# A planned order for windowed attention and a gated feed-forward layer: ScalarE's exponentials and tanh freed of each other, the plan's ranks searched again

## The chip, the cores and the metric

The kernel runs on one core of one Trainium2 chip. The metric is the device time of one execution in microseconds (us). A core has five engines that work at the same time, each through its own instructions in their given order: TensorE (PE in the profile, with PEld for its weight loads), VectorE (DVE), ScalarE (ACT), GpSimd (POOL) and SyncE (SP, which here issues the DMAs).

## The reference

Eight sequences of 576 tokens pass through attention with 8 heads of 64 and a window of 64 keys, and then through a feed-forward layer whose hidden part is gated by its own convolution.

```python
scores = scale * np.matmul(q, k.transpose(0, 1, 3, 2))
mask = (rel >= 0) & (rel < window)
scores = np.where(mask, scores, -1000000000.0)
attn = np.exp(scores - np.max(scores, axis=-1, keepdims=True))
attn = attn / (np.sum(attn, axis=-1, keepdims=True) + 1e-09)
x = np.matmul(attn, v)              # heads side by side: 512 columns
h = np.maximum(x @ w_in, 0.0)       # 512 -> 1024
conv_out = sum(conv_w[k] * hp[:, k:k + S, :] for k in range(3))
gate = 1.0 / (1.0 + np.exp(-conv_out))
return (h * gate) @ w_out           # 1024 -> 512
```

The weights come as 64-bit floats and are made into 32-bit ones on the chip. Each operand of the two large products is split into a high and a low part, and a product is made of three matmuls: high by high, low by high and high by low.

## The kernel before

**Units.** The 4608 tokens are cut into 12 units of 384 (`NU`, `NX`). A unit passes through attention (scores, exponentials, values), then the first product for 8 slices f of 128 hidden columns (`mm1`, line 547: 12 matmuls a slice), ReLU (lines 573 and 576), the convolution and its gate for pairs of slices (`conv_mid` 582, `conv_side` 589, `sig` 596, `gate` 601, `gate_hi` 613, `gate_lo` 616), and the second product (`mm2`, line 625: 9 matmuls a slice, three for each block of 128 tokens), after which the result is copied out of PSUM (lines 679 and 681) and stored.

**Attention.** `qk` (line 375) makes the scores with small matmuls on parts of the array; `row_max` (382, DVE) masks them and takes the maxima; `exps` (392, ACT) takes the exponentials with their sums; `guard`, `reciprocal` and `normalise` (395, 398, 403) divide. For units 0 and 1 the probabilities are transposed by PE (`transpose_pe` 408, copied out by `untile` 413), for the later ones by DVE (429) and DMAs (441). `values` (527) multiplies by v, again with small matmuls, one work for each of four slices c; `split_hi` (531, ACT) and `split_lo` (534, DVE) make the two parts that `mm1` reads.

**Weights.** w_in and w_out come in slices of 512 KB (line 273, into `bits`, which has four places). `to_f32` rebuilds a slice with ACT (259 and 264) and DVE (260, 261 and 265); `weights` then splits it (280 or 282, and 283). w_in is converted as slices 0, 1, (2,3), (4,5), (6,7), w_out as (0,1), (2,3), (4,5), (6,7).

**The planner.** The order on each engine isn't written out; `queued` (lines 67 to 143) works it out when the program is built. Every piece of work is a `Work` with an engine, a cost in us, what it reads and writes, and a rank `t`. The planner keeps a clock for each engine. At each step it takes the engine that can start first, and of that engine's ready works the one of lowest rank; a work of the same `kind` as the one before it on its engine counts as 0.5 lower. Ranks count steps of the first product: unit u's slice f has rank n = 8u + f, and a negative rank stands ahead of unit 0. Unit u's second product of slice f has rank n + lag + 0.5; each row of `START["sig"]`, `["pv"]`, `["qk"]` and `["ex"]` gives, relative to 8u, the ranks of unit u's gates, of unit u+1's values, and of unit u+2's scores and exponentials. The last row of each holds for all later units. The numbers in `START` are found by a search over the planner's clock, and they decide the order alone: on the chip, an engine goes on as soon as its next instruction's data is there.

**Kinds.** On PE the small matmuls of scores and values are "tiled" (units 0 and 1, and all values) or "eight" (scores from unit 2 on), and going in or out costs `SWITCH["PE"]` or `LEAVE`. On ACT, exponentials are of kind "exp" and tanh of kind "sig". A change costs 1.28 us on the planner's clock, and lines 741 to 745 add a name "table" to what these works read or write, so that no exponential crosses a tanh in either direction.

**Filling.** Where the planner sees PE idle before 110 us it adds matmuls on a zero tile (`keep_busy`, line 222), as many as fit in the gap by its clock. Their results are not used.

**The first loads.** `load_qk` for unit 0 issues four pairs of loads of k and q (two groups of heads g, each cut in two along the tokens, a = 0 and 1; line 245), all of one rank, `START["qk0"][0] - 1` = -98.8. The loads of ranks below that are w_in's slice 0 (-258.9) and the convolution's weights (-180.9, line 304).

Of the kernel before, what the change touches and what calls it, by code (L numbers as in the profile page):

```python
# [31 lines left out]
NB = 4  # L32
# [34 lines left out]
def queued(works, fill=None):  # L67
# [30 lines left out]
    dma, port, order, left = 0.0, {"DVE": 0.0, "POOL": 0.0}, [], len(works)  # L98
    while left:
# [29 lines left out]
        end = free[e] = start + turn + x.cost * (1.75 if e == "PE" and start < WARM else 1.0)  # L129
# [18 lines left out]
    "v0": -71.95,  # L148
    "pv0": -34.655,
    "conv": -180.897,  # L150
    "bits": ((-258.913, -43.524), (-27.85, -45.73)),
    "qk1": -49.157,
    "lag": (14.24, 14.398, 15.694, 15.676, 15.748, 15.604),
    "mid": (34.105, 23.924, 1.179, 2.877),
    "v1": -14.571,
    "qk2": 1.159,
    "qk0": (-97.809, -91.941, -91.937, -96.905, -77.255, -53.129),
    "ex0": (5.091, -53.0, -51.19, -48.925, -20.5, -38.281),
    "sc1": (-39.624, -39.363, -29.157, -27.618, -17.395, 0.944),
    "ex1": (-174.932, -9.707, -5.699, 0.394, -22.941, 2.774),  # L160
    "mask": -65.788,
    "sig": ((11.177, 14.758, 14.533, 18.236), (11.894, 12.691, 15.861, 19.769), (14.354, 16.018, 17.085, 17.977), (13.566, 14.937, 17.862, 18.669)),
    "in": (-109.707, -10.794, -9.091, -3.35, 0.324),
    "out": (1.022, 7.827, 9.957, 12.645),
# [9 lines left out]
COLD = 5.4  # L174


@with_exitstack
def attention_moe(ctx: ExitStack, tc: tile.TileContext, q, k, v, w_in, conv_w, w_out, out):
# [76 lines left out]
    def to_f32(t, n, st, x, kb, kt):  # L255
# [3 lines left out]
        at(t, "ACT", 0.0009 * n + 0.2, lambda: nc.scalar.activation(x, hw.bitcast(F32), AF.Abs, scale=2.0 ** -112), r=kb, w=kt)  # L259
        two(t, "DVE", 0.00052 * n + 0.06, lambda: nc.vector.tensor_scalar(xu, xu, 3, None, op0=ALU.logical_shift_left), w=kt)  # L260
# [3 lines left out]
        at(t, "ACT", 0.0009 * n + 0.2, lambda: nc.scalar.activation(lw, lw, AF.Copy, scale=2.0 ** -29), w=kb)  # L264
        two(t, "DVE", 0.00104 * n + 0.07, lambda: nc.vector.tensor_tensor(xu, xu, lw, ALU.add), r=kb, w=kt)  # L265

    def weights(t, src, fs, hi, lo, key, buf, halves):
# [11 lines left out]
        if key == "out":  # L279
            at(t, "ACT", 0.0009 * n + 0.12, lambda: nc.scalar.copy(hi, x), r=kt, w=his)  # L280
        else:
            two(t, "POOL", 0.00127 * n, lambda: nc.gpsimd.tensor_copy(hi, x), r=kt, w=his)
# [180 lines left out]
    def weigh(u, ns, t):  # L463

        bis = [divmod(2 * n + i, NB) for n in ns for i in range(2)]
        for b, i in bis:
            at(t, "ACT", 0.78, lambda b=b, i=i: exps(u, b, i), r=[("nm", b, i)], w=[("s", b, i), ("sm", b, i)], kind="exp")
# [5 lines left out]
        at(t, "DVE", 0.15, lambda: reciprocal(b, e), r=sw, w=[("r", b, i) for _, i in bis])  # L473
        two(t, "DVE", 0.05 + 0.275 * len(bis), lambda: normalise(u, b, e, nc.vector), r=[("r", b, i) for _, i in bis], w=sr)
        for n in ns:
            m, g = [("po", PE_AT[u][n])], 2 * n // NT
            at(t + 0.4, "PE", 0.66, lambda n=n: transpose_pe(u, n), r=[("s", b, n % 2 * 2), ("s", b, n % 2 * 2 + 1), "mask0"], w=m)
            at(t + 0.5, "ACT", 0.55, lambda n=n: untile(u, n), r=m, w=[("u", g, i) for i in range(4)])

    def softmax(u, b, t, ex_at):  # L480
# [18 lines left out]
        at(t, "DVE", 0.15, lambda: reciprocal(b, e), r=sw, w=[("r", b, i) for i in range(NB)])  # L499
# [217 lines left out]
    for u in range(NU):  # L717
# [4 lines left out]
        for c, x in enumerate(START["pv"][min(u, 3)]):  # L722
            attend(u + 1, c, n0 + x)
# [84 lines left out]
```

## Time and profile before

| | |
|---|---|
| median of 3 runs | 508.27 us (508.21 to 508.46) |
| profiled execution | 508.16 us |
| its span, first to last instruction | 506.4 us |
| granted TensorE clock, mean | 1.0 |
| read from and written to HBM | 47.73 and 9.44 MB, 113 GB/s over the span |

The span is what the trace covers. The profiled execution took 1.76 us more than its span and 0.11 us less than the median. In the rows, L547 is line 547 of the kernel; an entry such as "acc<-xh,wih" names what is written and what is read; "x384" is a count. A PE row "issue" is time in which PE waited for nothing that the profile shows.

### The profile page before, as it was taken

The numbers are of one execution on the slowest core, as the hardware profiler recorded it, in microseconds if no ns is written. First come the engines' busy times: TensorE is split into PE (matmuls) and PEld (weight loads), VectorE is DVE, ScalarE is ACT, GpSimd is POOL, SyncE is SP. The second block draws the span as 40 slices with busy tenths as digits, with TensorE's granted clock in tenths as the row PEclk, the third lists the DMA queues.
The fourth block names the chain that finished last, engine by engine and source line by source line (L and its number), as shares of the span: only waits on it lengthen the run. The fifth ranks groups of instructions, "written<-read, shape, count | busy, mean of one in ns | idle before, by whom it ended". The sixth has DMA issues, their size and how long they took to land.

```text
span 506.4 us, 14083 instructions
## 1 busy us (share of the span) xinstructions
PE 497.4 (98%) x5452; PEld 446.8 (88%) x5452; DVE 370.8 (73%) x1079; ACT 338.0 (67%) x975; POOL 94.1 (19%) x196
## 2 busy tenths in 40 slices
PE   8999999999999999999999998999999999999997
PEld 7888998988989989988989997998998998999886
DVE  4899999798687667767867666685877775454980
ACT  5999988768768648647747755854864864444750
POOL 7125412401121402102200400220220320000000
PEclk9999999999999999999999999999999999999999
DMA  8985833528128226316415522722720521100111
GB/s 294 380 312 204 329 119 112 222 73 322 32 64 293 79 64 244 113 48 212 160 48 168 195 57 82 274 54 81 276 61 15 190 66 29 63 0 1 63 63 62
DMA packets 28162, 69.88 MB, mean 138 GB/s; under 512 B 5696, under 2 KB 15680, under 8 KB 28096
## 3 DMA queue, kind: packets, MB, share of 16 engines
q1 hardware_dynamic: 27952, 68.86, 39.8%
q8 instruction: 43, 0.70, 0.6%
q14 instruction: 23, 0.19, 0.1%
q10 hardware_dynamic: 144, 0.13, 0.1%
HBM read 47.73 MB, written 9.44 MB: 113 GB/s over the span
## 4 chain that ended last, share of the span: by engine, by line
PE 91%; DVE 4%; ACT 2%; issue 1%; DMA 1%; SPq 0%; POOL 0%; ACTq 0%; POOLq 0%
PE acc L547 39%; PE po L625 39%; PE acc L527 7%; PE sc L375 3%; PE acc L375 2%; ACT s L392 2%; DVE s L382 1%; DMA q<-in_q_dram 1%; DVE T L261 1%; PE sc L625 1%; DVE T L265 0%; ACT ub L413 0%; DVE xl L534 0%; DVE T L260 0%; DVE wil L283 0%
## 5 line engine op out<-in xcount | busy, mean ns | idle before, releaser
L589 DVE SCALAR_TENSOR_TENSOR c<-hbuf,cw,c 128x384 f32<-128x384 f32 (+1 forms) x192 | 116.8, 659 | 28.2 <-ACT c L582 27.5
L547 PE MATMUL acc<-xh,wih 128*128 128x384 f32 x384 | 130.9, 341 | 1.0 <-DVE nm L382 1.0
L547 PE MATMUL acc<-xl,wih 128*128 128x384 f32 x384 | 129.4, 337 | 0.0
L547 PE MATMUL acc<-xh,wil 128*128 128x384 f32 x384 | 129.0, 336 | 0.0
L625 PE MATMUL po<-woh,gh 128*128 128x512 f32 (+1 forms) x288 | 113.3, 393 | 0.0
L625 PE MATMUL po<-wol,gh 128*128 128x512 f32 (+1 forms) x288 | 112.5, 391 | 0.0
L625 PE MATMUL po<-woh,gl 128*128 128x512 f32 (+1 forms) x288 | 111.1, 386 | 0.0
L392 ACT ACTIVATE s<-s,nm 128x96 f32<-128x96 f32 (+2 forms) x288 | 105.1, 371 | 3.9 <-DVE nm L382 3.9
L547 PEld LDWEIGHTS acc<-xh,wih 128*128 128x128 f32 x384 | 72.1, 188 | 6.1 <-DVE nm L382 1.0
L576 ACT ACTIVATE hbuf<-acc 128x384 f32<-128x384 f32 x64 | 31.3, 492 | 65.5 <-PE acc L547 65.5
L547 PEld LDWEIGHTS acc<-xh,wil 128*128 128x128 f32 x384 | 72.1, 188 | 2.7
L403 POOL TENSOR_TENSOR s<-s,r 128x768 f32<-128x768 f32 x27 | 42.9, 1590 | 159.7 <-DVE r L398 124.9
L547 PEld LDWEIGHTS acc<-xl,wih 128*128 128x128 f32 x384 | 72.1, 188 | 0.0
L625 PEld LDWEIGHTS po<-woh,gl 128*128 128x128 f32 x288 | 54.1, 188 | 11.8
L625 PEld LDWEIGHTS po<-woh,gh 128*128 128x128 f32 x288 | 54.0, 187 | 9.3
L625 PEld LDWEIGHTS po<-wol,gh 128*128 128x128 f32 x288 | 54.2, 188 | 7.3
L601 DVE SCALAR_TENSOR_TENSOR c<-c,hbuf 128x768 f32<-128x768 f32 (+1 forms) x48 | 50.3, 1048 | 11.8 <-ACT c L596 11.5
L582 ACT ACTIVATE c<-hbuf,cw 128x384 f32<-128x384 f32 (+1 forms) x96 | 53.7, 609 | 4.9 <-DVE gl L616 4.9
L392 ACT ACTIVATION_READ_ACCUMULATOR s<-s,nm 128x1 f32 x288 | 55.4, 192 | 0.0
L616 DVE TENSOR_TENSOR gl<-c,gh 128x768 fp32r<-128x768 f32 x48 | 45.6, 950 | 12.8 <-ACT gh L613 12.6
L613 ACT CAST gh<-c 128x768 fp32r<-128x768 f32 x48 | 39.9, 834 | 22.3 <-DVE c L601 13.4
L527 PEld LDWEIGHTS acc<-ub,v 128*64 128x64 f32 x1152 | 36.2, 138 | 8.3 <-issue 6.0
(76 smaller groups left out, 547.2 us busy)
## 6 DMA issues: line engine op xcount, KB each, us to landing
v<-in_v_dram SPq DMA_DIRECT2D x24, 768.0 KB, 6.2
ub<-T SPq DMA_DIRECT2D x240, 48.0 KB, 1.9
k<-in_k_dram SPq DMA_DIRECT2D x22, 448.0 KB, 6.3
q<-in_q_dram SPq DMA_DIRECT2D x22, 384.0 KB, 6.5
out_dram<-T SPq DMA_DIRECT2D x11, 768.0 KB, 3.6
bits<-in_w_in_dram SPq DMA_DIRECT2D x8, 512.0 KB, 8.2
bits<-in_w_out_dram SPq DMA_DIRECT2D x8, 512.0 KB, 4.8
k<-in_k_dram SPq DMA_DIRECT2D x2, 256.0 KB, 4.7
```

The lines of the kernel that those rows point to most:

```text
L375: nc.tensor.matmul(bank_of(u, b, i, h)[r:r + rows, o:n], qs[hs, 2 * g + p, t:t + rows], ks[hs, 2 * g + p, t + o:t + n], start=True, stop=True)
L392: nc.scalar.activation(x, x, AF.Exp, bias=nms[b][:, e], scale=-1.0, accum_out=sms[b][:, e])
L403: on.tensor_tensor(sv, sv, rs[b][:, e].unsqueeze(2).broadcast_to([P, e.stop - e.start, n]), ALU.mult)
L527: nc.tensor.matmul(acc[bank(("v", u, c))][h * D:(h + 1) * D, t * W:(t + 1) * W], vs[:, c, t, h], ub[g][:, 2 * p:2 * p + 2, 2 * t + h], sta ...
L547: nc.tensor.matmul(acc[bank(("m", u, f))][:, :NX], w[:, f, c], x[u % 2][:, c], start=(c == 0 and j == 0), stop=(c == NC - 1 and j == 2))
L576: nc.scalar.activation(hbuf[:, f, 1:1 + NX], ps[:, :NX], AF.Relu, scale=0.5)
L582: nc.scalar.activation(cs[i % 2][:, a, :n], hbufs[u % 2][:, f, 1:1 + n], AF.Copy, scale=cw[:, 1, f:f + 1])
L589: nc.vector.scalar_tensor_tensor(c, hbufs[u % 2][:, f, e:e + n], cw[:, e, f:f + 1], c, op0=ALU.mult, op1=ALU.add)
L601: nc.vector.scalar_tensor_tensor(c, c, 1.0, hbufs[u % 2][:, 2 * i:2 * i + 2, 1:1 + n], op0=ALU.add, op1=ALU.mult)
L613: nc.scalar.copy(halves(u, ghs[ring(u, i)]), kept(u, cs[i % 2]))
L616: nc.vector.tensor_tensor(halves(u, gls[ring(u, i)]), kept(u, cs[i % 2]), halves(u, ghs[ring(u, i)]).bitcast(F32), ALU.subtract)
L625: nc.tensor.matmul(ps[:, :e.stop - e.start], x, w[:, f, e], start=(f == 0 and j == 0), stop=(f == NF - 1 and j == 2))
```

## The change

It has four parts.

1. Exponentials and tanh lose their kinds. The 1.28 us for a change and the "table" dependencies are gone from the plan, so that exponentials, tanh and gates may stand in any order on ACT.
2. The planner's clock learns of PE's supply of instructions: small matmuls use up a store (`FEED`, `FEED_CAP`), which fills at `FEED_RATE`; a work that finds too little lasts longer on the planner's clock.
3. The four pairs of first loads of k and q get a rank each (`START["first"]`).
4. Costs of works are set to durations nearer to the trace, and all ranks are searched anew. `sig`, `pv`, `ex` and `qk` get a fifth row each and `mid` a fifth entry.

No work is added or taken away: each instruction of the reference's computation stays, in another place of its engine's order. The number of filling matmuls can change.

```diff
@@ queued
-    dma, port, order, left = 0.0, {"DVE": 0.0, "POOL": 0.0}, [], len(works)
+    dma, fed, fed_at = 0.0, FEED_CAP, 0.0
+    port, order, left = {"DVE": 0.0, "POOL": 0.0}, [], len(works)
...
-        end = free[e] = start + turn + x.cost * (1.75 if e == "PE" and start < WARM else 1.0)
+        end = start + turn + x.cost * (1.75 if e == "PE" and start < WARM else 1.0)
+        if e == "PE" and x.kind:
+            n, supply = FEED[x.kind] * x.cost, FEED_RATE if start < 95 else 3.0
+            fed = min(FEED_CAP, fed + (start - fed_at) * FEED_RATE)
+            end += max(0.0, (n - fed - supply * (end - start)) / FEED_RATE)
+            fed, fed_at = max(0.0, fed + (end - start) * supply - n), end
+        free[e] = end
@@ START
-    "v0": -71.95,
-    "conv": -180.897,
-    "bits": ((-258.913, -43.524), (-27.85, -45.73)),
-    "lag": (14.24, 14.398, 15.694, 15.676, 15.748, 15.604),
-    "mid": (34.105, 23.924, 1.179, 2.877),
-    "sig": ((11.177, 14.758, 14.533, 18.236), (11.894, 12.691, 15.861, 19.769), (14.354, 16.018, 17.085, 17.977), (13.566, 14.937, 17.862, 18.669)),
-    "in": (-109.707, -10.794, -9.091, -3.35, 0.324),
-    "out": (1.022, 7.827, 9.957, 12.645),
-    "pv": ((6.465, 3.218, 3.982, 6.814), (5.391, 7.651, 7.7, 7.657), (4.506, 6.705, 6.851, 6.707), (5.736, 6.769, 6.475, 6.894)),
-    "qk": ((4.51, 3.967, 5.895), (7.399, 7.175, 7.913), (5.253, 4.827, 5.309), (5.703, 5.416, 6.817)),
+    "v0": -96.077,
+    "first": (-137.786, -116.075, -136.572, -107.669),
+    "conv": -81.327,
+    "bits": ((-96.451, -86.268), (-79.16, -73.986)),
+    "lag": (14.497, 13.78, 14.414, 14.455, 15.373, 15.868),
+    "mid": (17.91, 0.125, 1.189, 3.534, 0.816),
+    "sig": ((12.866, 11.647, 14.331, 16.917), (12.693, 14.451, 17.624, 16.371), (12.581, 15.72, 15.39, 17.641), (12.826, 14.888, 15.551, 18.095), (11.686, 15.325, 16.648, 19.92)),
+    "in": (-24.305, -20.754, -9.713, -6.689, -3.697),
+    "out": (-2.439, -0.767, 9.791, 13.159),
+    "pv": ((3.969, 6.795, 4.159, 6.958), (7.28, 7.239, 7.367, 7.68), (6.46, 6.532, 6.657, 6.788), (6.325, 6.971, 6.181, 6.599), (6.49, 6.675, 6.478, 6.731)),
+    "qk": ((0.694, 3.909, 10.137), (7.309, 6.673, 8.272), (3.708, 3.714, 7.013), (2.788, 2.736, 6.609), (3.334, 3.026, 6.693)),
...
+FEED, FEED_CAP, FEED_RATE = {"tiled": 33, "eight": 78}, 150.0, 12.0
@@ load_qk
             for a in range(len(CUTS[g])) if u == 0 else (0,):
+                t = START["first"][2 * g + a] if u == 0 else t
@@ to_f32, weights: costs
-        at(t, "ACT", 0.0009 * n + 0.2, lambda: nc.scalar.activation(x, hw.bitcast(F32), AF.Abs, scale=2.0 ** -112), r=kb, w=kt)
-        two(t, "DVE", 0.00052 * n + 0.06, lambda: nc.vector.tensor_scalar(xu, xu, 3, None, op0=ALU.logical_shift_left), w=kt)
+        at(t, "ACT", 0.0009 * n + 0.11, lambda: nc.scalar.activation(x, hw.bitcast(F32), AF.Abs, scale=2.0 ** -112), r=kb, w=kt)
+        two(t, "DVE", 0.00045 * n + 0.08, lambda: nc.vector.tensor_scalar(xu, xu, 3, None, op0=ALU.logical_shift_left), w=kt)
...
@@ weigh (softmax in the same way)
-            at(t, "ACT", 0.78, lambda b=b, i=i: exps(u, b, i), r=[("nm", b, i)], w=[("s", b, i), ("sm", b, i)], kind="exp")
+            at(t, "ACT", 0.78, lambda b=b, i=i: exps(u, b, i), r=[("nm", b, i)], w=[("s", b, i), ("sm", b, i)])
...
@@ moe
-            s = n0 + START["sig"][min(u, 3)][i]
-            m = max(n + 0.4 if u % 3 == 2 else n + NF + 0.4, s - START["mid"][min(u, 3)])
+            s = n0 + START["sig"][min(u, 4)][i]
+            m = max(n + 0.4 if u % 3 == 2 else n + NF + 0.4, s - START["mid"][min(u, 4)])
...
-            at(s, "ACT", 0.75, lambda i=i: sig(u, i), w=[c], kind="sig")
-            two(s + 0.05, "DVE", 0.92, lambda i=i: gate(u, i), r=hs, w=[c])
+            at(s, "ACT", 0.75, lambda i=i: sig(u, i), w=[c])
+            two(s + 0.05, "DVE", 0.875, lambda i=i: gate(u, i), r=hs, w=[c])
...
@@ the plan's first lines
-    load_qk(START["qk0"][0] - 1, 0)
+    load_qk(None, 0)
```

The ranks of `qk0`, `ex0`, `sc1`, `ex1`, `pv0`, `v1`, `qk1`, `qk2` and `ex` change as well.

More of the change, by code (lines that the diff above doesn't have):

```diff
@@ L279, in weights @@
         if key == "out":
-            at(t, "ACT", 0.0009 * n + 0.12, lambda: nc.scalar.copy(hi, x), r=kt, w=his)
+            at(t, "ACT", 0.00088 * n + 0.05, lambda: nc.scalar.copy(hi, x), r=kt, w=his)
         else:
-            two(t, "POOL", 0.00127 * n, lambda: nc.gpsimd.tensor_copy(hi, x), r=kt, w=his)
+            two(t, "POOL", 0.00105 * n, lambda: nc.gpsimd.tensor_copy(hi, x), r=kt, w=his)
         two(t, "DVE", 0.00104 * n + 0.07, lambda: nc.vector.tensor_tensor(lo, x, hi.bitcast(F32), ALU.subtract), r=kt + his, w=los)
@@ L472, in weigh @@
         at(t, "POOL", 0.6, lambda: guard(b, e, nc.gpsimd), w=sw)
-        at(t, "DVE", 0.15, lambda: reciprocal(b, e), r=sw, w=[("r", b, i) for _, i in bis])
+        at(t, "DVE", 0.12, lambda: reciprocal(b, e), r=sw, w=[("r", b, i) for _, i in bis])
         two(t, "DVE", 0.05 + 0.275 * len(bis), lambda: normalise(u, b, e, nc.vector), r=[("r", b, i) for _, i in bis], w=sr)
@@ L477, in weigh @@
             at(t + 0.4, "PE", 0.66, lambda n=n: transpose_pe(u, n), r=[("s", b, n % 2 * 2), ("s", b, n % 2 * 2 + 1), "mask0"], w=m)
-            at(t + 0.5, "ACT", 0.55, lambda n=n: untile(u, n), r=m, w=[("u", g, i) for i in range(4)])
+            at(t + 0.5, "ACT", 0.47, lambda n=n: untile(u, n), r=m, w=[("u", g, i) for i in range(4)])
     def softmax(u, b, t, ex_at):
@@ L490, in softmax @@
             at(t, "ACT", 0.74, lambda b=b, i=i: exps(u, b, i), r=[("nm", b, i)],
-               w=[("s", b, i), ("sm", b, i)], kind="exp")
+               w=[("s", b, i), ("sm", b, i)])
         t += 0.45
@@ L498, in softmax @@
             at(t, "DVE", 0.15, lambda: guard(b, e, nc.vector), w=sw)
-        at(t, "DVE", 0.15, lambda: reciprocal(b, e), r=sw, w=[("r", b, i) for i in range(NB)])
+        at(t, "DVE", 0.12, lambda: reciprocal(b, e), r=sw, w=[("r", b, i) for i in range(NB)])
         if u < 3:
@@ L537, in attend @@
         g, x = c // 2, u % 2
-        at(t, "PE", 0.72, lambda: values(u, c), r=[("v", g)] + [("u", g, i) for i in range(4)], w=[("acc", ("v", u, c))],
+        at(t, "PE", 0.735, lambda: values(u, c), r=[("v", g)] + [("u", g, i) for i in range(4)], w=[("acc", ("v", u, c))],
            kind="tiled")
-        at(t + 0.1, "ACT", 0.4, lambda: split_hi(u, c), r=[("acc", ("v", u, c))], w=[("xh", x, c)])
+        at(t + 0.1, "ACT", 0.375, lambda: split_hi(u, c), r=[("acc", ("v", u, c))], w=[("xh", x, c)])
         at(t + 0.2, "DVE", 0.48, lambda: split_lo(u, c), r=[("acc", ("v", u, c)), ("xh", x, c)], w=[("xl", x, c)])
@@ L638, in moe @@
                    w=[("acc", ("m", u, f))])
-            at(n + 0.3, "ACT", 0.4, lambda f=f: relu(u, f), r=[("acc", ("m", u, f))], w=[("h", y, f)])
+            at(n + 0.3, "ACT", 0.385, lambda f=f: relu(u, f), r=[("acc", ("m", u, f))], w=[("h", y, f)])
             for o in range(TT):
@@ L678, in moe @@
             if o % 2 == 0 or u < 2:
-                at(t + 0.05 * o, "ACT", 0.55, lambda o=o: nc.scalar.copy(ot[:, o], po[o]), r=[("po", o)], w=ob)
+                at(t + 0.05 * o, "ACT", 0.475, lambda o=o: nc.scalar.copy(ot[:, o], po[o]), r=[("po", o)], w=ob)
             else:
-                at(t + 0.05 * o, "DVE", 0.65, lambda o=o: nc.vector.tensor_copy(ot[:, o], po[o]), r=[("po", o)], w=ob)
+                at(t + 0.05 * o, "DVE", 0.61, lambda o=o: nc.vector.tensor_copy(ot[:, o], po[o]), r=[("po", o)], w=ob)
             if u == LAST:
@@ L721, in attention_moe @@
             break
-        for c, x in enumerate(START["pv"][min(u, 3)]):
+        for c, x in enumerate(START["pv"][min(u, 4)]):
             attend(u + 1, c, n0 + x)
         if u + 2 < NU:
-            for b, (x, y) in enumerate(zip(START["qk"][min(u, 3)], START["ex"][min(u, 3)])):
+            for b, (x, y) in enumerate(zip(START["qk"][min(u, 4)], START["ex"][min(u, 4)])):
                 softmax(u + 2, b, n0 + x, n0 + y)
```

26 lines of the change are left out of this document (13 added, 13 removed), and 2 rows, old and new, of the table START.

## The prediction

> **What bounds the kernel now.** I read the page's busy shares and slices first, then the busy times by stretch, then the chain of work that ended last.
>
> ```profile
> PE 497.4 (98%) x5452; PEld 446.8 (88%) x5452; DVE 370.8 (73%) x1079; ACT 338.0 (67%) x975; POOL 94.1 (19%) x196
> ...
> DVE  4899999798687667767867666685877775454980
> ```
>
> PE is busy 98% of the span of 506.4 us, and DVE only 73%, but DVE's slices (12.66 us each) stand at 9 from the third to the seventh. So the start has another limit than the rest. The stretches show it; behind each window and its length stand the busy us of PE, PEld, DVE, ACT and POOL:
>
> ```profile
> 7.00:25.00 18.00, 17.70 (x273) 15.83 (x274) 15.80 (x67) 16.47 (x61) 6.10 (x24) 1.00 1.02 386
> 25.00:47.00 22.00, 20.44 (x387) 17.72 (x387) 21.89 (x101) 20.86 (x73) 8.30 (x11) 1.00 0.74 256
> 47.00:90.00 43.00, 42.52 (x534) 39.07 (x536) 42.90 (x102) 38.57 (x105) 12.33 (x21) 1.00 0.57 198
> 90.00:105.00 15.00, 15.00 (x93) 14.16 (x89) 11.07 (x37) 11.03 (x40) 5.81 (x8) 1.00 0.50 174
> 320.00:460.00 140.00, 139.98 (x1300) 126.28 (x1299) 93.55 (x228) 84.00 (x224) 19.61 (x42) 1.00 0.28 91
> ```
>
> And two of the stretches for line 222 alone, the filling matmuls:
>
> ```profile
> 7.00:25.00 18.00, 8.47 (x62) 7.33 (x62) 1.00 1.02 386
> 25.00:47.00 22.00, 2.24 (x12) 1.70 (x12) 1.00 0.74 256
> ```
>
> From 7 to 47 us PE is idle 0.30 + 1.56 = 1.86 us and fills 8.47 + 2.24 = 10.71 us: 12.6 us without real work. From 320 to 460 it is idle 0.02 us of 140. The work of PE is fixed, so what can be won lies before 47 us, and in single gaps. In the start DVE sets the pace: between 25 and 90 us it is idle 0.11 + 0.10 = 0.21 us of 65. Only behind 90 us is it loose (3.93 us idle of 15). PE runs through from 47 us on because the first products of units 0 and 1 lie ready; it meets DVE again where the second product begins:
>
> ```profile
> 74.89 0.66 DVE L260 TENSOR_SCALAR T<-T 128x1024 uint32<-128x1024 uint32 x1
> ...
> 76.35 0.93 DVE L616 TENSOR_TENSOR gl<-c,gh 128x768 fp32r<-128x768 f32 x1
> 77.18 1.22 DVE L261 SCALAR_TENSOR_TENSOR T<-bits,T 128x1024 uint32<-128x1024 uint32 x1
> ...
> 80.71 1.23 DVE L265 CUSTOM_DVE_ANT_0 T<-bits,T 128x2048 uint16<-128x2048 uint16 x1
> ...
> 83.77 1.24 DVE L283 TENSOR_TENSOR wol<-T,woh 128x1024 fp32r<-128x1024 f32 x1
> ```
>
> ```profile
> 78.37 2.06 PE po L625 x9
> ...
> 105.22 2.06 PE po L625 x9
> ```
>
> The first gate is done at 76.35 + 0.93 = 77.28, and the chain of waits has its matmuls at 78.37: 1.1 us of slack. An earlier PE is worth nothing unless DVE delivers earlier too.
>
> **The change part by part.** *First loads.* The SP queue and the end of the first wait:
>
> ```profile
> 0.74 0.38 SPq L273 DMA_DIRECT2D bits<-in_w_in_dram  x1
> 1.18 0.41 SPq L304 DMA_DIRECT2D cbits<-in_conv_w_dram  x1
> 1.64 0.43 SPq L245 DMA_DIRECT2D k<-in_k_dram  x1
> 2.12 0.47 SPq L245 DMA_DIRECT2D q<-in_q_dram  x1
> ```
>
> ```profile
> 2.12 4.14 DMA q<-in_q_dram
> ...
> 6.39 0.56 PE sc L375 x16
> ```
>
> The new ranks put g0's first pair ahead (-137.8), then g1's first pair (-136.6), then the second pairs, then w_in's slice 0 (-96.45), v, and the rest. The first q takes SP's second place: issued at about 1.2 instead of 2.12, 0.9 us earlier. It also has less ahead of it: no 512 KB of weights. Those landed, issued at 0.74, when ACT began on them:
>
> ```profile
> 4.27 0.67 ACT L259 ACTIVATE T<-bits 128x512 f32<-128x512 f32 x1 [2.25 <-DMA bits<-in_w_in_dram]
> ...
> 4.97 0.43 DVE L260 TENSOR_SCALAR T<-T 128x512 uint32<-128x512 uint32 x1 [3.97 <-ACT T L259]
> ...
> 5.46 0.68 DVE L261 SCALAR_TENSOR_TENSOR T<-bits,T 128x512 uint32<-128x512 uint32 x1
> ...
> 7.82 0.75 DVE L265 CUSTOM_DVE_ANT_0 T<-bits,T 128x1024 uint16<-128x1024 uint16 x1
> ```
>
> That is 3.5 us from issue. k and q of the first pair are smaller, so I take 3.4, a landing at 4.6 instead of 6.26: 1.6 us won (bounds 0.9, the issue alone, and 2.1). In return slice 0's conversion loses its place. It now runs in DVE's empty time before the scores; its rank goes from -109.7 to -24.3, between the first exponentials. DVE's 0.43 + 0.68 + 0.75 = 1.86 us then fall where it has 18.00 - 15.80 = 2.2 us of idle time (7 to 25 us), which may or may not lie in the right places: cost 0 to 1.9, taken as 0.9, the middle, since I see nothing that decides. Net: **-0.7 us**, bounds -2.1 and +1.0.
>
> *The order on DVE and ACT to 105 us.* The last conversion of w_out (the four rows of 74.89 to 83.77) takes 0.66 + 1.22 + 1.23 + 1.24 = 4.35 us of DVE and is done at 85.01, yet its slices 6 and 7 are first used at 105.22. In the old ranks it (12.645) stands ahead of the tanh of unit 0's second pair (14.758); in the new ones that tanh (11.647) stands ahead of it (13.159). This is where the freed order counts: tanh need not stand behind exponentials of lower rank. Moving those 4.35 us behind what PE waits for could win up to 3.9 us, the room that DVE has from 90 to 105. Against it: w_out's first two conversions go from 1.022 and 7.827 to -2.439 and -0.767, which brings DVE work ahead that no PE work before 78 us needs. The first of them is early already:
>
> ```profile
> 55.20 1.18 DVE L283 TENSOR_TENSOR wol<-T,woh 128x1024 fp32r<-128x1024 f32 x1
> ```
>
> It ends 22 us ahead of its use; so I let half of one conversion (2.2 us) be the loss at worst. I take **-2.5 us**, nearer to the first end, since the last conversion stands 20 us too early in the rows and PE's 12.6 us leave room for it; bounds -3.9 and +2.2. The other moved ranks of the start, those of the second unit's softmax and of the later loads on SP among them, are inside these bounds: the DMA engines are full from 7 to 25 us (share 1.02) and no longer behind (0.74), and the one wait for weights by ACT is the 2.25 us above. The freeing itself takes no instruction away: the chip changes no tables.
>
> ```profile
> L259 ACT ACT_TABLE_LOAD x1 | 1.3, 1283 | 0.7 <-PEq L797 0.7
> ```
>
> One load of 1283 ns serves all exponentials and tanhs, so the planner's 1.28 us for each change was never there to win.
>
> *Spacings on PE.* Two gaps of the chain fall inside bursts of small matmuls:
>
> ```profile
> 54.44 0.35 issue
> ...
> 307.27 1.31 issue
> ```
>
> At 307 us a softmax's pair of score works (128 matmuls) and one values work (24) run in one burst, and it stops at its end; at 54 us it is 72 and 64. The new clock charges for such bursts and the ranks are searched under that charge. I take **-1.5 us** of the 1.66, bounds -1.66 and 0; the other side is a rival. The stops go with the supply of instructions:
>
> ```profile
> q8 instruction: 43, 0.70, 0.6%
> ```
>
> Here the Trainium skill (Runtime: NRT & Kernel Launch, Instruction fetch mechanics) says that instructions come in blocks of 16 KiB (256 instructions), and that crossing into the next is mostly hidden. The block agrees: 0.70 MB in 43 packets is 16 KB, and twice 5452 PE rows over 43 is 254. That it is hidden holds for most bursts here, but not for the 1.31 us; by the Trainium skill's page alone this term would be 0 and the sum 1.5 us higher.
>
> *Costs and filling.* The new costs change only the order, and most come near to the rows: ACT's 512-wide conversion goes from 0.66 to 0.57 and its row lasts 0.67 with an overlap of about 0.1 into the next. Fewer or more filling matmuls cost PE nothing where it has nothing else; in a gap that closes early they delay real work by some tenths, bounds 0 and +0.5, taken as 0.
>
> Sum: -0.7 - 2.5 - 1.5 = -4.7 us. Against the profiled execution's 508.16 (span 506.4 and 1.76 around it) that gives 503.46, and against the median of 508.27, 503.57; I say **503.5**.
>
> **The rivals.** *DVE stays the limit.* Its work is the same, and in its idle first 7 us it loses slice 0; then the early loads and the order win nothing and only the gaps go: 508.27 - 1.66 = 506.6. For it speaks the 0.21 us of idle time in 65; against it, that 4.35 us of this work are demonstrably early. Chance 0.2, and about a third of that within 0.2% of no change.
>
> *All of it is won.* The near bounds of all terms hold: -2.1 - 3.9 - 1.66 = -7.7 us, 500.6, and 498 if another 2.6 of PE's 12.6 us close. Nothing in the rows forbids it; DVE would have to run nearly without a hole from the first scores on. Chance 0.12.
>
> *The bursts starve, slower.* In the new last rows the four values works of a unit (6.478 to 6.731) and the third score work (6.693) lie together: unit 4's second product stands, two units on, at f + 15.373 + 0.5 - 16, so at 5.87 and 6.87, and the first product at 6.01 and 7: a burst of 4 x 24 + 64 = 160 matmuls, where now there are 152 and 136. If each such burst of units 4 to 9 stops as that of 307 us does, 6 x 1.31 = 7.9 us are added where none is saved: 508.27 - 3.2 + 7.9 = 513.0. It decides from the point where 160 is more than the supply carries, and 152 was, once. Against it: the values go first and slowly,
>
> ```profile
> 352.63 2.32 PE L527 MATMUL acc<-ub,v 128*64 128x64 f32 x72
> ```
>
> 72 in 2.32 us, so the supply has longer to follow than with 128 score matmuls first; and the chain has no other "issue" of over 0.5 us behind 95 us. Chance 0.08.
>
> *Slice 0 and the early w_out delay the softmaxes, slower.* +1.0 + 2.2 - 1.5 = +1.7: 510.0. It decides once DVE loses more than the 1.1 us of slack ahead of 78.37. Chance 0.1.
>
> **How the numbers follow.** Forecast (501 to 506): 0.5. With the rivals' 0.2, 0.12, 0.08 and 0.1 this is 1.0. A measurement of this kernel can tell about 0.2%, 1.0 us. Faster: 0.5 + 0.13 + 0.12 = 0.75; same: 0.06 from the first rival and 0.04 from the mildest part of the last: 0.10; slower: 0.15. The range 497.5 to 509.5 leaves out the starved bursts, half of the last rival and a little at the low end.
>
> **What would show it.** Right: the first scores near 4.8 us; line 222's and the idle time's 12.6 us between 7 and 47 us shortened by 2 to 4; the first second-product matmuls 3 to 4 us before 78.37; the last w_out conversion behind the second gate; no row "issue" of over 0.5 us behind 95 us. Wrong: DVE idle between 25 and 70 us, a first gate at 77 or later, or repeated gaps before the scores of units 4 to 9. The prediction would fail by size most of all in the order's term, which I could bound but not follow instruction by instruction.

## The result, and the profile after

The changed kernel takes **505.22 us** (median of 6 runs, 504.55 to 506.74) where the kernel before took 508.30 (508.21 to 508.52) beside it: a ratio of 0.9942 with a 95% interval of 0.9929 to 0.9955, so 3.1 us or 0.6% faster. The profiled execution took 505.23 us, of which its span is 503.4. In this trace the lines behind the planner's new code stand 9 or 10 lower: the first product is L557, the second L635, the scores L385, the filling matmuls L231.

The same stretches as before the change, with busy us of PE, PEld, DVE, ACT and POOL:

```profile
7.00:25.00 18.00, 16.05 (x257) 13.91 (x257) 15.51 (x66) 16.13 (x56) 6.29 (x22) 1.00 1.02 396
25.00:47.00 22.00, 20.98 (x333) 18.32 (x330) 21.97 (x96) 22.00 (x80) 6.34 (x11) 1.00 0.77 274
47.00:90.00 43.00, 42.62 (x599) 38.67 (x598) 42.90 (x102) 38.52 (x104) 15.99 (x23) 1.00 0.56 189
90.00:105.00 15.00, 15.00 (x200) 13.95 (x199) 14.00 (x68) 12.88 (x51) 6.01 (x8) 1.00 0.44 156
```

And the first two of them for the filling matmuls alone:

```profile
7.00:25.00 18.00, 6.05 (x47) 5.26 (x45) 1.00 1.02 396
25.00:47.00 22.00, 3.11 (x22) 2.68 (x22) 1.00 0.77 274
```

PE's idle and filling time from 7 to 47 us is 1.95 + 1.02 + 6.05 + 3.11 = 12.1 us, hardly less than the 12.6 of before. DVE is still without a hole from 25 to 90 us, and it now does 14.00 us of work from 90 to 105 instead of 11.07. PE's timeline shows the start:

```profile
4.31 0.70 PE L385 MATMUL sc<-k,q 64*64 64x64 f32 x16
...
6.01 0.59 PE L385 MATMUL sc<-k,q 64*64 64x64 f32 x16
...
7.95 0.73 PE L385 MATMUL po<-k,q 64*64 64x128 f32 x17 [0.50 <-DMA q<-in_q_dram]
...
21.70 0.41 PE L557 MATMUL acc<-xh,wih 128*128 128x384 f32 x1 [0.53 <-DVE xl L544]
```

The first scores stand at 4.31 instead of 6.39. The first product begins at 21.70 instead of 24.36, the second at 75.32 instead of 78.21. The chain of waits shows where DVE lets go of PE, first before, then after:

```profile
46.75 0.14 issue
46.89 4.41 PE acc L547 x24
51.29 2.25 PE acc L527 x72
```

```profile
86.33 0.47 DVE xl L544
...
87.67 0.47 DVE xl L544
...
88.67 0.09 issue
88.77 0.92 PE acc L537 x24
...
236.58 0.36 issue
```

Before, the chain runs over DVE up to 46.75 us and then on PE alone. A busy DVE behind that point set no time: it was full from 47 to 90 us, and the chain did not pass through it. After, PE comes earlier, and the chain stays with DVE to 88.67 us. What PE loses to DVE there is little, though. Between 45 and 120 us it waits only twice for more than a moment (us in total, times, longest), the first time at 88.7 us, the second at 45:

```profile
PE acc L537 <- DVE c L599: 0.3, 1, 0.3
PE acc L557 <- DVE nm L392: 0.2, 1, 0.2
```

The stop of 1.31 us at 307 us is gone; a stop of 0.36 us stands at 236.6.

How far each kernel is can be counted at one instant, in rows of PE. A matmul of the two products gives one row, one of scores, values or filling two; numbers of scores and values in this section and in bursts below are rows. When 120 us have passed, both have begun 276 matmuls of the first product and 384 of the values. The kernel after has begun 81 of the second product instead of 75, and 728 of the scores instead of 768. By the chain's row "2.06 PE po L625 x9" a second-product matmul takes 0.229 us, and by the score rows below (60 in 0.93 us) a score matmul at most 0.0155. That is 6 x 0.229 - 40 x 0.0155 = 0.75 us of lead, nearer to 0.8 since the ends of score matmuls overlap. Of the 2.95 us by which the spans differ (506.39 and 503.44), **0.8 are won by 120 us, and 2.15 behind it**, where PE waits for no other engine.

### The profile page after: what moved, and what is told of

It is laid out like the page before. It is cut to its first block, busy times and chain, and to the rows that moved or that the text cites. A ratio compares the mean times of both kernels' runs of the same rounds, so it can differ in the third digit from the quotient of the medians.

```text
span 503.4 us, 14054 instructions
## 1 busy us (share of the span) xinstructions
PE 495.3 (98%) x5444; PEld 444.6 (88%) x5444; DVE 373.8 (74%) x1079; ACT 338.2 (67%) x975; POOL 93.8 (19%) x196
## 4 chain that ended last, share of the span: by engine, by line
PE 82%; DVE 12%; ACT 3%; issue 1%; DMA 1%; SPq 0%; POOL 0%; ACTq 0%
PE po L635 38%; PE acc L557 34%; PE acc L537 6%; PE sc L385 3%; DVE s L392 2%; DVE T L275 2%; DVE s L413 1%; DVE T L271 1%; PE acc L385 1%; ACT s L402 1%; DVE c L599 1%; DMA q<-in_q_dram 1%; DVE wol L293 1%; DVE xl L544 1%; DVE T L270 1%
## 5 line engine op out<-in xcount | busy, mean ns | idle before, releaser
L599 DVE SCALAR_TENSOR_TENSOR c<-hbuf,cw,c 128x384 f32<-128x384 f32 (+1 forms) x192 | 115.3, 651 | 26.4 <-ACT c L592 26.1
L557 PE MATMUL acc<-xh,wih 128*128 128x384 f32 x384 | 130.7, 340 | 1.0 <-DVE xl L544 0.5
L557 PE MATMUL acc<-xl,wih 128*128 128x384 f32 x384 | 129.5, 337 | 0.0
L557 PE MATMUL acc<-xh,wil 128*128 128x384 f32 x384 | 128.9, 336 | 0.0
L635 PE MATMUL po<-woh,gh 128*128 128x512 f32 (+1 forms) x288 | 113.4, 394 | 0.0
L635 PE MATMUL po<-wol,gh 128*128 128x512 f32 (+1 forms) x288 | 112.5, 391 | 0.0
L635 PE MATMUL po<-woh,gl 128*128 128x512 f32 (+1 forms) x288 | 111.2, 386 | 0.0
L557 PEld LDWEIGHTS acc<-xh,wih 128*128 128x128 f32 x384 | 72.1, 188 | 6.5 <-POOL s L467 0.7
L557 PEld LDWEIGHTS acc<-xh,wil 128*128 128x128 f32 x384 | 72.1, 188 | 3.0
L557 PEld LDWEIGHTS acc<-xl,wih 128*128 128x128 f32 x384 | 72.0, 188 | 0.0
L626 DVE TENSOR_TENSOR gl<-c,gh 128x768 fp32r<-128x768 f32 x48 | 52.0, 1085 | 20.3 <-ACT gh L623 20.1
L635 PEld LDWEIGHTS po<-woh,gl 128*128 128x128 f32 x288 | 54.1, 188 | 11.8
L611 DVE SCALAR_TENSOR_TENSOR c<-c,hbuf 128x768 f32<-128x768 f32 (+1 forms) x48 | 47.4, 990 | 21.6 <-ACT c L606 21.3
L635 PEld LDWEIGHTS po<-woh,gh 128*128 128x128 f32 x288 | 54.0, 187 | 10.4
L635 PEld LDWEIGHTS po<-wol,gh 128*128 128x128 f32 x288 | 54.2, 188 | 7.4
L413 POOL TENSOR_TENSOR s<-s,r 128x768 f32<-128x768 f32 x27 | 41.3, 1530 | 78.3 <-DVE r L408 57.8
L606 ACT ACTIVATE c<-c 128x768 f32<-128x768 f32 (+1 forms) x48 | 40.4, 844 | 6.3 <-DVE c L599 5.7
```

What stands on the lines that cost most here:

```text
L413: on.tensor_tensor(sv, sv, rs[b][:, e].unsqueeze(2).broadcast_to([P, e.stop - e.start, n]), ALU.mult)
L557: nc.tensor.matmul(acc[bank(("m", u, f))][:, :NX], w[:, f, c], x[u % 2][:, c], start=(c == 0 and j == 0), stop=(c == NC - 1 and j == 2))
L599: nc.vector.scalar_tensor_tensor(c, hbufs[u % 2][:, f, e:e + n], cw[:, e, f:f + 1], c, op0=ALU.mult, op1=ALU.add)
L606: nc.scalar.activation(c, c, AF.Tanh)
L611: nc.vector.scalar_tensor_tensor(c, c, 1.0, hbufs[u % 2][:, 2 * i:2 * i + 2, 1:1 + n], op0=ALU.add, op1=ALU.mult)
L626: nc.vector.tensor_tensor(halves(u, gls[ring(u, i)]), kept(u, cs[i % 2]), halves(u, ghs[ring(u, i)]).bitcast(F32), ALU.subtract)
```

## The experiments

All reorderings are made behind the planner, on the finished queue of each engine: `behind(works, y)` and `ahead(works, y)` put works of one engine directly behind or ahead of y. Each run stands beside the kernel before on the same chip, whose median was 508.0 to 508.6.

**Bursts.** A burst is a run of small matmuls (scores and values) between large ones, and a stop is time inside it in which PE waits for nothing that the profile shows. In the kernel before, the values work that follows two score works goes behind the next half of a first product (b_split). In the kernel after, the third score work, behind four values works, goes behind the next three works (a_split).

```diff
 # b_split
+        for i, x in enumerate(pe):
+            if x.kind == "tiled" and x.t > 20 and pe[i - 1].kind == pe[i - 2].kind == "eight" and not pe[i + 1].kind:
+                products = [y for y in pe[i + 1:] if y.w[0][0] == "acc"]
+                behind([x], products[0])
 # a_split
+            if x.kind == "eight" and x.t > 10 and [y.kind for y in pe[i - 4:i]] == ["tiled"] * 4:
+                behind([x], pe[i + 3])
```

> The kernel before with one thing moved: wherever its planned order on PE has a single values work (24 matmuls) right behind two score works (128 matmuls), that values work goes behind the next half of a first product; nothing else moves. If long bursts of small matmuls starve PE of instructions, the stop of 1.31 us at 307 us goes and the time falls from 508.3 to about 506.9. If that stop came from something else (a load of k and q was issued at the same moment, 306.5 us), it stays or turns up elsewhere: 508.3 within 0.3.

> The changed kernel with one thing moved: wherever four values works (96 matmuls) are followed by the third score work (64 matmuls), the score work goes behind the next three second-product works (2.06 us). Starving theory: the two excesses of the changed kernel in those bursts (about 0.67 us at 236 and 0.2 us at 271 us) go, the time falls from 505.2 to about 504.3, and its spread over the runs (504.55 to 506.74) narrows to that of the kernel before (0.3 us). Rival, the bursts of 160 are harmless and the spread has another source: 505.2 and the same spread. If the later scores hold up VectorE and then PE, the time rises by 1 us or more.

b_split: 509.20 beside 508.04, ratio 1.0024 (1.0011 to 1.0038). a_split: 506.38, ratio 0.9964 (0.9951 to 0.9978), some 1.1 us above the kernel after by the two ratios, whose intervals just overlap; the span of its trace is 504.4 us, 1.0 above. In both traces the stop that was aimed at is gone, and in neither is its time won. In a_split the whole 1.0 us is lost behind 117 us. b_split is another case. Its order on PE is that of the kernel before up to 150 us, and yet its trace is 1.3 us late from 56 us on, because a score work waits for a q that landed late:

```profile
PE sc L375 <- DMA q<-in_q_dram: 1.9, 1, 1.9
```

That loss is none of the edit's. From the burst that ends at 121 us to the end (119 in the kernel before) b_split takes 387.1 us and the kernel before 387.0, although the stop is gone. In both runs each burst that is cut in two adds a change of kind on PE, whose kinds are large matmuls, scores and values. The rows show the price. Each pair below is the start of the same score work of two units that follow each other, with 96 first-product, 72 second-product, 96 values and 192 score matmuls between them; kernel before, kernel after, a_split:

```profile
304.75 0.93 PE L375 MATMUL acc<-k,q 64*32 64x96 f32 x60
...
345.73 0.93 PE L375 MATMUL acc<-k,q 64*32 64x96 f32 x60
...
385.17 0.93 PE L375 MATMUL acc<-k,q 64*32 64x96 f32 x60
```

```profile
332.91 0.93 PE L385 MATMUL acc<-k,q 64*32 64x96 f32 x60
...
372.25 0.93 PE L385 MATMUL acc<-k,q 64*32 64x96 f32 x60
```

```profile
333.71 0.93 PE L385 MATMUL acc<-k,q 64*32 64x96 f32 x60
...
373.24 0.93 PE L385 MATMUL acc<-k,q 64*32 64x96 f32 x60
```

A unit takes 39.44 us before (6 changes of kind), 39.34 after (5), 39.53 in a_split (6): 0.1 to 0.2 us for a change. The first pair, with the stop, takes 40.98: the stop costs its unit 1.5 us. The values give the price once more. In the row of 51.29 above 72 of them take 2.25 us in the kernel before, and after

```profile
116.86 2.95 PE acc L537 x96
```

so 24 cost 0.70 and the beginning of a burst of values 0.15. Behind 110 us the kernel before has 49 changes of kind and the kernel after 41. Six of the eight lie between scores and values; between large and small matmuls it is 34 and 32.

**Where the stops stand.** Counting all rows of PE and PEld in order from 0, semaphore rows too, every stop of over 0.5 us in these traces is at row 193 of a block of 256. A few repeated score matmuls early on move all later rows against the blocks: 13 in the kernel before (b_shift), 9 in the kernel after (a_shift), each with two rows of PE and two of PEld.

```diff
+        again([x for x in order if x.eng == "PE" and x.t == START["qk0"][5]][0], 13)   # 9 in a_shift
```

> The kernel before with 13 small matmuls of unit 0's last score work done twice, a shift by 52 places. Block theory: the stops at 54.8 us (0.35 us) and 307.3 us (1.31 us) go, since their bursts no longer hold two boundaries, and a new one can appear near 109 us, where a burst of 24 and 128 small matmuls now holds two; so the stops move with the stream and the time falls by 0.4 to 1.6 us. Rival, they hang on what the DMA engines carry at those times: the stops stay at 54.8 and 307.3 us and the time stays within 0.3 us.

> The changed kernel with 9 small matmuls of unit 0's last score work done twice (the same result again), which shifts PE's later instructions by 36 places in its stream; no order changes. Theory: PE's instructions come in blocks of 256, and a burst of small matmuls stops PE only when it holds two block boundaries with mostly score matmuls between them. In the changed kernel that is the burst at 232.7 us alone, and the shift takes its second boundary away: no stop in PE's second half, and the time is lower by 0.4 to 0.9 us than the changed kernel's on the same chip (about 1.0 to 1.3% below the kernel before: 0.5 us of it uncertain, since the chips differ), with a spread below 1 us. Rival, stops depend on the load of the DMA engines alone: a stop of 0.3 us or more stays near 236 us.

b_shift: 508.10 beside 508.18, ratio 0.9997 (0.9986 to 1.0007); the stop at 307 us is gone, and another has come at 229, again at row 193. The one at 54 us is at the same row as before, so at another matmul, and has grown from 0.35 to 1.37 us:

```profile
54.28 1.37 issue
```

```profile
229.31 0.98 issue
```

a_shift: 505.02, ratio 0.9940 (0.9924 to 0.9956); its trace has no stop behind 95 us, and its span of 503.3 is near the 503.4 of the kernel after, since the repeated matmuls, a wait for q longer by 0.2 us and some stops of under 0.2 us cost about what the stop had. So a stop moves with the count of instructions ahead of it. That the new ranks avoid the one at 307 us is partly a matter of alignment.

**DVE's pace.** Three runs on the kernel before: w_out's last conversion (4.35 us of DVE, and two works of ACT) behind unit 2's last `split_lo`, at about 93 us (b_wout); 16 small fills on DVE at 31 us (b_dve31); the same at 67 us (b_dve67).

```diff
 # b_wout
+        late = [x for x in order if x.t == START["out"][3] and (x.eng == "DVE" or x.eng == "ACT" and ("w24", 1, 0) not in x.w)]
+        behind(late, xls[-1])
...
 # b_dve31; b_dve67 has "out2l"
+        more([x for x in order if x.eng == "DVE" and "in2l" in x.w][0])   # 16 x nc.vector.memset(pad, 0.0), 128x120
```

> The kernel before with only w_out's last conversion (slices 6 and 7: four VectorE works of 4.35 us in all, and two ScalarE works) moved behind the last low part of unit 2's x, at about 93 us. The prediction's step on the order: 2.5 us won, at most 3.9, so 505.8 (504.4 at best). Rival: behind 47 us PE waits for nobody in the kernel before, so time freed on VectorE at 75 to 85 us buys nothing: 508.3 within 0.3.

> The kernel before with 16 more small VectorE instructions (memsets of a tile that nothing reads) behind the low part of w_in's slices 2 and 3, at 31 us; about 1.8 to 2.6 us of VectorE. If VectorE sets the pace of the start, the time rises by nearly all of it, +1.5 to +2.6. If PE's end hangs on other things there (filling matmuls still stood at 29 and 39 us), by less than 0.5.

> The kernel before with 16 fills of 128x120 added on DVE at about 67 us, which took 3.9 us of DVE at 31 us and cost 4.0 there. Theory of the record (DVE sets the pace until 105 us): +3.9 again, a ratio of 1.0076. Rival (PE no longer waits for DVE behind 47 us, as the conversion moved away from there showed; DVE is then ahead of PE by about 1.1 us at the first gate): +2.0 to +2.8, 1.004 to 1.0055. Rival 2 (DVE has room behind 47 us for all of it): within 0.1%.

b_wout: 510.27 beside 508.04, ratio 1.0041 (1.0026 to 1.0055), no gain. b_dve31: 512.02, ratio 1.0074 (1.0059 to 1.0089), 4.0 us for fills that hold DVE for 3.9 us (16 of 0.158 us, and the gaps between them). b_dve67: 511.01 beside 508.08, ratio 1.0054 (1.0040 to 1.0067), 2.9 us for the same fills. What PE waited for in b_dve31 and in b_dve67 (us in total, times, longest; lines 10 lower than in the kernel before):

```profile
PE po L385 <- DVE nm L392: 3.1, 1, 3.1
```

```profile
PE acc L557 <- ACT hbuf L583: 1.4, 1, 1.4
...
PE po L635 <- DVE gl L626: 0.7, 1, 0.7
```

At 31 us DVE sets the pace one to one. At 67 us it is about 1 us ahead of PE (3.9 - 2.9): work added there costs all but that, and work taken away wins nothing. b_wout shows the second half, but its 2.2 us are no price of the move alone. In its trace PE is 1.5 us late at the first second-product matmul (79.74 instead of 78.21) and still 1.5 us late at the 193rd of the first product (93.36 instead of 91.83), so nothing was won where DVE had been relieved. Of these 1.5 us, 1.1 are a larger stop at 54 us, ahead of anything that was moved. Behind 93 us the moved works hold up ACT, which stands 3.81 us before its copy of w_out, and PE waits for a ReLU:

```profile
PE acc L547 <- ACT hbuf L576: 1.3, 1, 1.3
```

**The first loads, undone in the kernel after.** w_in's slice 0 and the convolution's weights are loaded first again (a_first); then also slice 0's conversion stands at the head of ACT and DVE again (a_first_conv).

```diff
 # a_first
+        ahead([weights0, conv], first[0])
 # a_first_conv, besides
+        ahead(early, queue["ACT"][0])
+        ahead(early, queue["DVE"][0])
```

> The changed kernel with the loads of w_in's slice 0 and of the convolution's weights issued first again, as before; nothing else moves. If the earlier k and q carry to the end through VectorE's full stretch, as the prediction's 1.6 us supposes, the time rises by 1.2 to 2.0 us. If VectorE's and ScalarE's holes in the first 22 us swallow it, by less than 0.5 us.

> As the run with the old first loads, and slice 0's conversion (two ScalarE and three VectorE instructions) back at the head of both engines, as before. The prediction's net of this pair of edits was 0.7 us (bounds 2.1 and -1.0): the time rises by 0.7 us over the changed kernel. If the exchange was worth nothing, within 0.3 us of it; if the conversion had better stayed early, it falls.

a_first: 508.31 beside 508.18, ratio 1.0001 (0.9990 to 1.0012): the whole gain is gone. a_first_conv: 507.97, ratio 0.9995 (0.9985 to 1.0005). By these two alone the first loads would be the whole gain. The next runs tested that.

**The first loads, made in the kernel before** (b_first), and **q issued from ACT's queue** in the kernel after (a_qact):

```diff
 # b_first
+        behind([x for x in sp if x.w in ([("bits", 0, 0)], ["cbits"])][:2], loads[-1])
+        behind(a[:1], exs[6])      # a, d: slice 0's works on ACT and DVE
+        behind(a[1:], ups[0])
+        ahead(d[:1], nrm[0])
+        behind(d[1:2], nrm[0])
+        behind(d[2:], nrm[2])
...
 # a_qact
+                    by = nc.scalar if u == 0 and name == "q" else nc.sync
```

> The kernel before, with the first loads of k and q ahead of those of w_in's slice 0 and the convolution's weights, and slice 0's conversion (4 works on ACT and DVE, the copy on POOL) moved behind the first softmaxes, as in the kernel after; everything else stays. Theory (the pair of loads and conversion is the gain, and it doesn't depend on the new order): undoing it in the kernel after cost 2.8 us, so here it gains 2.3 to 2.8: 505.3 to 505.8 where before is 508.1, a ratio of .9945 to .9955, with the first scores near 4.4 instead of 6.4. Rival 1 (the record's sum): -0.7, a ratio of .9986. Rival 2 (the pair pays only with the new piece order and the freed softmaxes; the undoing cost 2.8 because the order of after is built on early loads): within 0.2% of before.

> The kernel after, with the four first loads of q issued from ACT's queue instead of SP's, so that k and q are issued side by side: the second q leaves at about 1.3 instead of 2.24 us, the fourth at 2.5 instead of 4.29; the table load of 1.28 us moves behind them, to about 2.8 to 4.1. Theory (the issue on one queue, 0.5 us for each load, is the term that sets the first scores, and each us won there is worth about one at the end): first scores at about 3.8 to 4.0, the third score work at 7.0 to 7.4 instead of 7.95, the time 0.5 to 1.0 us under the kernel after: 504.1 to 504.7 where before is 508.1, a ratio near .9925. Rival 1 (the transfers set the landing: 4.55 us from issue to landing at a DMA share of 0.9): the third score work stays at 7.9 and the time that of after, .9942. Rival 2: the table load behind the issues delays the first exponential past 5.45 us: slower than after by up to 0.5.

b_first: 512.95 beside 508.08, ratio 1.0092 (1.0077 to 1.0107), 4.9 us slower, with the first scores where they were:

```profile
1.05 5.46 PE L222 MATMUL acc<-spare 128*128 128x112 f32 x24 [1.05 <-DVE spare L225]
6.44 0.57 PE L375 MATMUL sc<-k,q 64*64 64x64 f32 x16
```

The kernel before has 12 filling matmuls ahead of the first scores (24 rows), the kernel after 7. In b_first the early data stood behind the 12. The first product began at 29.3 instead of 24.4; that the conversion, moved late, did the rest is likely (PE waits 2.5 us for the softmax on DVE) but was not tried apart. a_qact: 505.72, ratio 0.9947 (0.9932 to 0.9963), no better than the kernel after. Issued side by side, the larger loads of k and q (256 KB) took 6.2 and 6.6 us to land instead of 4.3 and 4.8: the transfers set the landing there, not the queue.

**Filling.** The last run is a_first with 12 filling matmuls ahead of the first scores instead of 7, and nothing else.

```diff
+        fills = queue["PE"][0]
+        do = fills.do
+        fills.do = lambda: (do(), keep_busy(5, ("acc", 0))())
```

> The kernel with w_in's slice 0 and the convolution's weights loaded first again (as in the run that undid only this, 508.3 beside 508.1 for before), and 12 instead of 7 filling matmuls ahead of the first scores, as many as in the kernel before: PE has then nothing to wait for until about 5.7 us, when the first q lands. In the run without them PE stood idle for 1.36 us, and the next eight entries of filling took 2.05 us instead of 1.15. Theory W (of the 3.1 us that undoing the order of the loads costs, 1.45 is the later landing and about 0.9 is a PE that has grown slow in the wait; the prediction's price for the landing, 1.6, was then near, and what it lacked is the slow stretch): the eight entries take 1.15 to 1.3 us, the second score work starts at 7.4 to 7.8 instead of 8.57, the first product at about 23.1 instead of 24.0, and the time is 507.2 to 507.5 where before is 508.1, a ratio near .9985. Rival L (the landings alone set all of it; a fuller PE changes nothing): second scores still at 8.4 or later, first product at 24.0, ratio 1.000. Rival F (five more fills stand in the way): first scores behind 6.0, ratio above 1.0005.

It takes 505.96 beside 508.63, a ratio of 0.9945 (0.9931 to 0.9958): five matmuls whose results nobody reads bring back some 2.8 us, by the two ratios (1.0001 and 0.9945), and 2.0 between the two traces. PE's timeline in a_first, then in a_first_fill:

```profile
1.05 3.33 PE L231 MATMUL acc<-spare 128*128 128x112 f32 x14 [1.05 <-DVE spare L234]
5.75 0.92 PE L385 MATMUL sc<-k,q 64*64 64x64 f32 x16 [1.36 <-DMA q<-in_q_dram]
6.59 2.05 PE L231 MATMUL acc<-spare 128*128 128x112 f32 x8
8.57 0.92 PE L385 MATMUL sc<-k,q 64*64 64x64 f32 x16
```

```profile
1.05 5.46 PE L231 MATMUL acc<-spare 128*128 128x112 f32 x24 [1.05 <-DVE spare L234]
6.57 0.56 PE L385 MATMUL sc<-k,q 64*64 64x64 f32 x16
7.07 1.15 PE L231 MATMUL acc<-spare 128*128 128x112 f32 x8
8.14 0.56 PE L385 MATMUL sc<-k,q 64*64 64x64 f32 x16
```

In a_first PE runs out of work at 4.4 us and waits 1.36 us; the next eight rows take 2.05 us instead of 1.15. The second score work comes later in a_first (8.57) than in a_first_fill (8.14), though the first one came earlier. Three traces of one order can be compared at fixed points, since they differ only in their start:

| starts at, us | after | a_first_fill | a_first |
|---|---|---|---|
| first product | 21.70 | 23.27 | 24.02 |
| 49th matmul of the first product | 45.41 | 46.99 | 47.74 |
| unit 3's values | 116.79 | 118.14 | 119.27 |
| last matmul of the second product | 499.80 | 500.60 | 502.60 |

What is lost by the first product is still lost at the 49th matmul: 1.58 us by later loads, another 0.75 by a slow PE. By unit 3's values the 1.58 have become 1.35, since the kernel after waits 0.3 us for DVE at 88.7 us and a_first_fill doesn't; the 0.75 have become 1.13, with a wait of 0.5 us for a DMA at 91 us in a_first. At the end a_first_fill is only 0.8 us behind the kernel after and 2.0 ahead of a_first. Some 0.7 to 0.8 us of both is luck: the five matmuls have moved the blocks, and the stop that stands at 236 us after, and at 239 in a_first, is missing. The same unit takes 37.88 us in the kernel after and 37.22 in a_first_fill:

```profile
218.31 0.93 PE L385 MATMUL acc<-k,q 64*32 64x96 f32 x60
...
256.19 0.93 PE L385 MATMUL acc<-k,q 64*32 64x96 f32 x60
```

```profile
219.60 0.93 PE L385 MATMUL acc<-k,q 64*32 64x96 f32 x60
...
256.82 0.93 PE L385 MATMUL acc<-k,q 64*32 64x96 f32 x60
```

That is 0.66 us; in a_first the unit takes 38.04 us, 0.82 more. By the two ratios the kernel after and a_first_fill are 0.0003 apart, inside both intervals, so at the end the price of the loads can't be told from 0. By unit 3's values it is 1.35 us.

The experiments gave no version that beats the kernel after.

## Why the prediction was right in sign and too large in size

Forecast 503.5, measured 505.22, inside the range. The whole hides that two terms were too small and the largest had the wrong sign. In the profiled runs, one execution of each kernel, the terms come out so:

| term | predicted | in the traces | from |
|---|---|---|---|
| first loads | -0.7 | -1.35 | unit 3's values, after against a_first_fill |
| order to 105 us | -2.5 | +0.55 | rest of the -0.8 at 120 us |
| bursts | -1.5 | -2.15 | spans less the lead at 120 us |
| sum | -4.7 | -2.95 | |

**First loads: the mechanism was right, the size was not.** The first q lands 2.4 us from issue, at 3.60 us instead of 6.25, where the prediction put 3.4 us and 4.6. These 2.65 us are more than its upper bound of 2.1. They do not all arrive: the first scores, behind 7 filling matmuls, come 2.08 us earlier, the third score work waits 0.50 us for its own q, and 1.58 us reach the first product. That this is near the 1.6 put for the landing is luck. The 0.9 us charged for slice 0's conversion between the exponentials is what wasn't there: put back at the head, in a_first_conv, it made the first product later, not earlier (24.7 beside 24.0), and the time moved by 0.3 us, within both intervals. That such a move can cost a lot is true all the same: in b_first a badly placed conversion and the 12 filling matmuls together cost 4.9 us.

**The order's term is the step that failed.** It said that between 25 and 90 us DVE sets the pace because it is idle for only 0.21 us of 65. Half of that holds. At 31 us it does (b_dve31). Behind 46.75 us the chain of waits of the kernel before has no DVE in it, and that row was there to be read before the change: busy isn't the same as waited for. Relieving DVE of w_out's last conversion there wins PE nothing, as b_wout shows up to 93 us. Nor did the new ranks move it far. In the kernel after, two of its four DVE works still stand ahead of the second gate's end at 79.10, where three did before, and it is done at 83.86 instead of 85.01:

```profile
73.82 0.68 DVE L270 TENSOR_SCALAR T<-T 128x1024 uint32<-128x1024 uint32 x1
...
76.16 1.21 DVE L271 SCALAR_TENSOR_TENSOR T<-bits,T 128x1024 uint32<-128x1024 uint32 x1
78.19 0.91 DVE L626 TENSOR_TENSOR gl<-c,gh 128x768 fp32r<-128x768 f32 x1
79.03 1.21 DVE L275 CUSTOM_DVE_ANT_0 T<-bits,T 128x2048 uint16<-128x2048 uint16 x1
...
82.64 1.22 DVE L293 TENSOR_TENSOR wol<-T,woh 128x1024 fp32r<-128x1024 f32 x1
```

The prediction's own sentence, that an earlier PE is worth nothing unless DVE delivers earlier too, then met the new kernel: with PE earlier, the chain stays with DVE until 88.67 us, and PE waits 0.3 us for it there, which is about what the loads' 1.58 us lose on the way to 1.35. Where the order's own +0.55 comes from wasn't tried and stays open.

**The bursts' term was near by two errors.** The stop at 307 us went, 1.5 us, and a smaller one at 188 us with it, 0.12 of PE's idle time; but a new one at 236 costs its unit 0.66, and b_shift shows how little the avoided stop says about the ranks: that much of the gain is luck. What the step lacked is the number of changes of kind: 41 instead of 49 behind 110 us, at 0.1 to 0.2 us each 0.8 to 1.6 us; 2.15 - 1.5 - 0.12 + 0.66 leaves 1.2 for them and for stops too short to be told apart. That is the plan's grouping of values and scores, which a_split undoes in part and loses 1.0 us by, and b_split cuts further and so gets nothing for the stop that it removes.

**Costs and filling, put at nothing,** hide a price where PE has not yet run long enough: with 7 filling matmuls instead of 12 ahead of late data, PE loses another 0.75 us by the first product. The kernel after has 7 and early data, and that suits it; early data behind 12 (b_first) or late data behind 7 (a_first) doesn't pay. **The freed kinds** took away no instruction, as said (one table load in both profiles); freeing them alone wasn't tried, so what the freedom is worth to the new order isn't shown.

**The rivals.** That DVE stays the limit was right for the chain up to 88.67 us of the kernel after, though not for the time. The starved bursts of 160 did appear, values first; of the six only one stopped for more than 0.3 us, at 236. That slice 0 and the early w_out delay the softmaxes has the sign of the order's term, +0.55, but not its size, and a_first_conv speaks against slice 0 as the cause, if only with late loads. All of it was not won.

**The signs.** First scores near 4.8: 4.31. First second-product matmul 3 to 4 us earlier: 75.32 instead of 78.21 by PE's timeline, just short of it, and most of that lead was lent by other work, as the count at 120 us shows. The last conversion behind the second gate: half of it. No "issue" over 0.5 us behind 95 us: the longest is 0.36. The 12.6 us of idle and filling time shortened by 2 to 4: by 0.5 only, and this was the sign of the failed step.

## What to carry to other kernels

An engine that is busy without a hole sets the pace only as far as the chain of waits runs over it; look there for the last step at which it releases the bound engine, and price what taking work off it wins only ahead of that. Behind it added work can still cost, as soon as the slack is gone. Matmuls without use ahead of the first data are part of the change when loads are moved: count them, since too many stand in the way and too few leave PE slow. Undoing one part of a change can cost as much as the whole change wins and still not be its cause, if the undone part meets a plan made for the other: make the part alone as well, and repair the meeting point before you attribute.

## What was not expected of the hardware

**A slow PE at a granted clock of 1.00.** In a_first the first 14 filling rows take 3.33 us (0.24 each), later groups of 22 take 2.71 (0.12 each), while the granted clock reads 1.00 in both stretches, 0 to 7 and 7 to 25 us. With a wait of 1.36 us at 4.4 us PE is slow until about 9.4, where the second score work ends; in a_first_conv, with a wait of 1.98, beyond 11 us. Without a wait the slow stretch ends earlier, at about 4.5 us in the kernel after and by an estimate from its 24 rows in 5.46 us at about 6.2 in a_first_fill. The Trainium skill (TensorE: Matmul & The Clock Gate, Part 1: The HAM clock gate) says that the array runs at half rate until it has been busy for a window of some 3.4 us, and that the window's place against the kernel's start varies. The factor of two agrees, and so does a_qact, where PE does the same work up to the first scores as in the kernel after and the next eight rows take 1.55 us instead of 1.15. With one trace of each run, how much of a_first's slow stretch is the wait and how much the place of the window isn't shown.

**Stops at the 256th instruction.** The stops at 54 and 307 us (before), 236 (after), 54 and 229 (b_shift) all lie at row 193 modulo 256 of PE and PEld, in bursts of small matmuls, and take 0.35 to 1.4 us. What decides whether a crossing stops PE stays open: some bursts with a crossing run through, and the same matmul in the same order is held up by 0.35 us at 54 us in the kernel before and by 1.44 in b_wout. The Trainium skill (Runtime: NRT & Kernel Launch, Instruction fetch mechanics) calls the crossing mostly hidden; that holds for most of them here.

**A change between kinds of matmul costs 0.1 to 0.2 us** (39.34, 39.44 and 39.53 us for one unit with 5, 6 and 6 changes, and 0.15 for the beginning of a burst of values); eight fewer of them are worth nearly as much as the stop at 307 us. The Trainium skill (TensorEngine Tiling (Array Packing), Key Properties) says that a change of the tiling mode drains TensorE; the trace agrees, and has the price that the page doesn't give.
